# Attention of two blocks as one piece of work: pair tiles, one operation for both, another order of steps

## The chip, the cores and the metric

The kernel runs on one NeuronCore of a Trainium2 chip. The core has a matrix engine (TensorE, PE in the profile; PEld is its weight loading), three elementwise engines (VectorE = DVE, ScalarE = ACT, GpSimd = POOL), and SyncE (SP), which here issues every DMA, in program order. Each engine works through its own list in order and waits on semaphores. The metric is the device time of one launch in microseconds (us), lower is better.

## What is computed

A gated linear attention recurrence, and after it a feed-forward layer with squared ReLU, all in float32:

```python
# q, k, v, alpha: (B=4, H=8, S=768, D=48)
state = zeros(B, H, D, D)
for t in range(S):
    state = alpha[:, :, t, :, None] * state + einsum('bhd,bhe->bhde', k[:, :, t], v[:, :, t])
    y[:, :, t] = einsum('bhd,bhde->bhe', q[:, :, t], state)
x = y.transpose(0, 2, 1, 3).reshape(B * S, H * D)      # 3072 x 384
h = maximum(x @ w_in, 0)                               # w_in 384 x 2048, given as float64
out = h * h @ w_out                                    # w_out 2048 x 384, given as float64
```

## The kernel before

**Blocks and groups.** The sequence is cut into chunks of 128 steps; one chunk of one batch is a block. There are 24 blocks, block `n` being chunk `n // 4` of batch `n % 4`. Four blocks make a group (`GB = 4`), so six groups of 512 rows, and the feed-forward layer is computed group by group.

**Attention of a block.** `ln` takes the logarithm of alpha (ScalarE), from block 8 on `sp` splits it into two parts, `cs` sums along the chunk with a triangular matrix (TensorE), `eb` and `ei` exponentiate the sums with both signs (ScalarE), `mq` and `mk` scale q and k with them (VectorE), `turn` transposes both (TensorE) and `qc`, `kc` copy the result out (ScalarE). Then `scores` (L418) multiplies them in quarters of the array, `masked` (L426) keeps the lower triangle in a tile `am`, `state_sums` (L441) forms the products of k and v, and `sums_copied` (L452) makes `us`, the state at the middle of the chunk. `next_state` (L466, L467) makes the state for the next chunk; it needs `last`, the decay over the whole chunk, one column per head. From block 4 on `bl` stores the last row of the exponentials to DRAM and `br` fetches it back turned into columns, both by DMA; for blocks 0 to 3 `lt` and `lc` do it on TensorE and VectorE. The output products `y` (L398) come in two parts, `ga` and `gb`, since rows of the array change PSUM banks between them; `ev` copies y into `x` (L562).

**Pairs.** From block 4 on blocks go in pairs, with three short stretches of 64-wide matmuls between the layer's 128-wide ones: `turn` for both; `ga`: scores and sums of the first block, then the first part of the products of the pair before; `gb`: the second part of those products, then scores and sums of the second block. PSUM has eight banks, handed out in turn to all of these and to the layer's sums.

**The layer.** Group 0 multiplies float32 data directly (`ffn_in`, L931; L760 with `w_out`). Later groups use three passes over reduced-precision parts of weights (`wb`, `wl`, `wd`) and data (`xa`, `xl`, `xd`; `ha`, `hl`, `hd`): `in_x`, `in_y` (L681), then `turned_x`, `turned_y` (L843, L855) or `out_x`, `out_y` (L760). `splits_of_x` makes the parts of x in three column pieces. The parts `wl` and `wd` are kept in DRAM and streamed back by `pump` (L644) as long as fewer than `room` tiles are held.

**Weights.** They arrive as 64-bit floats in 16 pieces and are turned into float32 by `convert_first`, `convert_middle`, `convert_second` (L174 to L203).

**The order.** The first 30 us are a list written out by hand (`first`, L980): each word is a step and its block. `zeros2` (L384) is three matmuls on zeros whose result is not used, and `warm` (L244) is one more of that kind. `weights` loads the next piece of weights. `gt`, `gy`, `gk` hold the next load back until the transposes, the products or the sums of that block are done. After it, `weave` runs a list of units (layer matmuls, with a cost in units of its own) and slips in events at given times; `PLAN` (L996) gives the times of the attention steps within a pair, and `AT` (L19) every other constant. All of this fixes the order in which each engine and the DMA queue see their work.

## Time and profile before

| what | value |
|---|---|
| time, median of 3 runs | 516.4 us (515.83 to 516.55) |
| profiled execution, span from first to last instruction | 514.6 us |
| TensorE, weight load, VectorE, ScalarE busy | 508.3, 404.6, 377.0, 302.3 us |
| group 0, from the start to the first pass of group 1 | 0 to 124.5 us |
| groups 1 to 5, start of each | 124.5, 212.3, 291.7, 370.3, 444.9 us |
| last matmul of the chain ends | 510.9 us |
| DMA | 102.73 MB, mean 200 GB/s |
| granted TensorE clock | 1.00 |

The profile page gives busy times per engine, a chain of waits (what released what, followed back from the last instruction), and groups of equal instructions. A line of the chain or the timeline reads: start in us, length in us, engine, line of the kernel, what was written and read, how many. A bracket at its end is the idle time of that engine before it and who ended it. A float32 matmul leaves two records, so 16 score matmuls are 32.

### The profile page before, as it was taken

Reading aid. Unit: us, or ns where it says so; the run is one execution under the profiler, and the core shown is the slowest. Engines: PE = TensorE matmul, PEld = TensorE weight load, DVE = VectorE, ACT = ScalarE, POOL = GpSimd, SP = SyncE. Lnnn points to the kernel's source line nnn. Section 1 sums busy time; section 2 is a strip of 40 time slices with the busy share of each in tenths; the row PEclk is TensorE's granted clock in tenths of the full one; section 3 lists DMA queues with packets and bytes.
Section 4 is the critical chain, followed back from the end, with each engine's and each line's share of the span. In section 5 each row is a group of like instructions: output and inputs, shape, how many; then the busy total and the mean of one; then the engine's idle time right before and its main releaser. Section 6 shows DMA issues by size and latency. Waiting matters only on the chain.

```text
span 514.6 us, 12773 instructions
## 1 busy us (share of the span) xinstructions
PE 508.3 (99%) x5166; PEld 404.6 (79%) x5166; DVE 377.0 (73%) x656; ACT 302.3 (59%) x627; POOL 6.0 (1%) x33
## 2 busy tenths in 40 slices
PE   8999999999999999999999999999999999999997
PEld 6884456669877679988888888888888888888996
DVE  3798899898789869886698286799275588274961
ACT  4789875677788576376764175855075663144520
POOL 4000000000000000000000000000000000000000
PEclk9999999999999999999999999999999999999999
DMA  9989867272797788799975678894775544789201
GB/s 171 226 238 269 233 177 226 33 224 101 267 238 199 189 188 234 263 330 222 241 187 154 209 220 229 222 225 146 227 221 168 186 128 151 214 277 401 88 0 63
DMA packets 144794, 102.73 MB, mean 200 GB/s; under 512 B 116560, under 2 KB 118240, under 8 KB 144736
## 3 DMA queue, kind: packets, MB, share of 16 engines
q1 hardware_dynamic: 144736, 101.92, 70.4%
q8 instruction: 41, 0.67, 0.6%
q14 instruction: 17, 0.14, 0.1%
HBM read 84.57 MB, written 17.33 MB: 198 GB/s over the span
## 4 chain that ended last, share of the span: by engine, by line
PE 96%; DMA 2%; SPq 1%; DVE 1%; issue 0%; ACT 0%; DVEq 0%; POOLq 0%
PE h L681 31%; PE o L760 22%; PE o L843 13%; PE h L931 8%; PE o L855 6%; PE y L398 4%; PE sckv L418 3%; PE T L529 2%; PE sckv L441 2%; PE cs L288 1%; DMA a_in<-in_alpha_dram 1%; PE zeros L384 1%; DMA last<-row 1%; PE cs L291 1%; SPq L333 1%; PE cs L292 1%
## 5 line engine op out<-in xcount | busy, mean ns | idle before, releaser
L696 ACT ACTIVATE hid<-h 128x512 f32<-128x512 f32 x56 | 33.7, 601 | 88.4 <-PE h L681 86.7
L681 PE MATMUL h<-xd,wd 128*128 128x512 f32 x240 | 68.4, 398 | 0.0
L681 PE MATMUL h<-xa,wb 128*128 128x512 f32 x240 | 67.8, 391 | 0.0
L681 PE MATMUL h<-xl,wl 128*128 128x512 f32 x240 | 67.6, 390 | 0.0
L594 DVE TENSOR_TENSOR hid<-h,hid 128x512 f32<-128x512 f32 x56 | 38.5, 689 | 33.9 <-PE h L681 33.6
L562 ACT COPY x<-y 32x256 f32<-32x256 f32 (+1 forms) x137 | 48.9, 365 | 8.7 <-PE y L398 6.4
L681 PEld LDWEIGHTS h<-xl,wl 128*128 128x128 f32 x240 | 45.0, 188 | 9.6
L681 PEld LDWEIGHTS h<-xa,wb 128*128 128x128 f32 x240 | 44.9, 188 | 9.4
L681 PEld LDWEIGHTS h<-xd,wd 128*128 128x128 f32 x240 | 43.7, 188 | 9.2
L760 PE MATMUL o<-w_out,hid 128*128 128x384 f32 x144 | 48.9, 492 | 0.0
L931 PE MATMUL h<-x,w_in 128*128 128x512 f32 (+1 forms) x120 | 43.0, 511 | 0.0
L655 ACT ACTIVATE ha<-hid 128x512 fp32r<-128x512 f32 x42 | 26.7, 638 | 26.1 <-DVE hx L656 12.8
L760 PEld LDWEIGHTS o<-w_out,hid 128*128 128x128 f32 x144 | 26.7, 190 | 17.2
L710 DVE SCALAR_TENSOR_TENSOR hid<-hid 128x512 f32<-128x512 f32 x56 | 37.8, 684 | 0.0
L931 PEld LDWEIGHTS h<-x,w_in 128*128 128x128 f32 x120 | 22.4, 190 | 16.9 <-issue 13.9
L855 PE MATMUL o<-hd,wd 128*128 128x512 f32 x144 | 33.4, 391 | 0.0
L656 DVE SCALAR_TENSOR_TENSOR hl<-ha,hid 128x512 fp32r<-128x512 f32 x42 | 28.8, 686 | 4.7 <-ACT ha L655 4.4
L855 PEld LDWEIGHTS o<-hd,wd 128*128 128x128 f32 x144 | 26.8, 188 | 6.1 <-ACT o L848 0.6
L594 DVE TENSOR_TENSOR hd<-ha,hl 128x512 fp32r<-128x512 f32 x42 | 29.1, 692 | 1.9
L843 PE MATMUL o<-hx,wb 128*128 128x512 f32 x72 | 28.4, 394 | 0.0
L843 PE MATMUL o<-hx,wl 128*128 128x512 f32 x72 | 28.0, 389 | 0.0
L843 PE MATMUL o<-ha,wb 128*128 128x512 f32 x72 | 28.0, 389 | 0.0
(130 smaller groups left out, 950.4 us busy)
## 6 DMA issues: line engine op xcount, KB each, us to landing
wd<-do SPq DMA_DIRECT2D x37, 384.0 KB
wl<-lo SPq DMA_DIRECT2D x34, 384.0 KB
wl<-li SPq DMA_DIRECT2D x32, 384.0 KB
wd<-di SPq DMA_DIRECT2D x32, 384.0 KB
raw<-in_moe_w_in_dram SPq DMA_DIRECT2D x8, 768.0 KB
raw<-in_moe_w_out_dram SPq DMA_DIRECT2D x8, 768.0 KB
v_in<-in_v_dram SPq DMA_DIRECT2D x24, 192.0 KB
a_in<-in_alpha_dram SPq DMA_DIRECT2D x22, 192.0 KB
```

What stands on the lines that cost most here:

```text
L398: ins = nc.tensor.matmul(out=ys[e][64 * half : 64 * half + D + G * e, m % 2, p // 2, t], lhsT=lhsT, rhs=rhs, start=(half, e) not in seen, ...
L562: copy(out=x[kk][to : to + m, t : t + 2], in_=blk[n]["y"][e][r : r + m, :, p // 2],)
L594: nc.vector.tensor_tensor(out=o, in0=x, in1=z, op=op)
L655: nc.scalar.activation(out=a, in_=x, func=AF.Copy, scale=NEAR * E)
L656: nc.vector.scalar_tensor_tensor(out=l, in0=a.bitcast(FP32), scalar=-1.0 / E, in1=x, op0=ALU.mult, op1=ALU.add)
L681: nc.tensor.matmul(out=acc["h", j], lhsT=here[w, "i", p][:, kk, jj * 128 : (jj + 1) * 128], rhs=x_parts[x][:, kk], start=start and kk == 0 ...
L696: nc.scalar.activation(out=hid[j], in_=x, func=AF.Copy, scale=E)
L710: nc.vector.scalar_tensor_tensor(out=h, in0=h, scalar=0.0, in1=h, op0=ALU.max, op1=ALU.mult)
L760: nc.tensor.matmul(out=acc[t][:, 0:DM], lhsT=lhs[:, t * C : (t + 1) * C], rhs=rhs, start=start, stop=stop, skip_group_check=True,)
L843: nc.tensor.matmul(out=acc[c], lhsT=by_parts(here[w, "o", p], jj, c), rhs=x, start=n == 0 and w == "b", stop=n == NJ - 1 and w == "l", ski ...
L855: nc.tensor.matmul(out=acc[c], lhsT=by_parts(here["d", "o", p], n % 2, c), rhs=h_diff[n], start=False, stop=last and n == NJ - 1, skip_gro ...
L931: nc.tensor.matmul(out=ps, lhsT=w[:, kk, c0 : c0 + 128], rhs=xT[g][kk][:, cols], start=(kk == 0), stop=(kk == KM - 1),)
```

## The change

- The tiles of alpha, q, k and v hold two blocks side by side, as do the states (`s_two`), `us` (`u_two`) and the exponentials (`wide`, tags `b` and `i`, one buffer each, shared with the split parts of the logarithms).
- From block 4 on one operation serves both blocks of a pair: `pair_ln`, `pair_sp`, `pair_mq`, `pair_mk`, `pair_bl` and `pair_br` (one store and two fetches for each pair), `pair_masked`, `pair_states`.
- `ga` now does the scores and masks of both blocks and the first part of the products; `gb` the sums of both blocks, the second part of the products, and then the states of both.
- The sums of odd heads use 48 columns of k, where it was 64. States and `us` are handled on 112 partitions.
- The list `first` has another order and no `zeros`. `mq`, `mk`, scores and sums stay one block at a time there, and `us` is a copy, since the state before chunk 0 is zero. `st1` stands earlier, `v2` and `v3` are loaded after the second piece of weights. The marks stand before other loads: `gt1` (the transposes of block 1) now holds back the first piece of weights (before: `v2`), `gy0` (the products of blocks 0 and 1) the third piece (before: `v3`), `gk3` (the sums of block 3) `q4` (before: the third piece).
- `split_x` and `diff_x` treat all three column pieces in one operation.
- `PLAN` and `AT` have other times and constants; the pool `wt` has 25 buffers in place of 26, `room` is 24 in place of 26 and `room1` 24 in place of 25. `EARLY`, a second plan for blocks 4 to 7, is gone.
- Assertions (`needs`, `done`) on the order run while the program is built, not on the chip. `JOINED` is 0, so that what hangs on it isn't used.

The diff, cut to its core:

```diff
--- before.py
+++ after.py
-AT = {'u0': 2, 'evs': 0.4, 'lead': 4, 'post': 3, 'w_first': (45.82, 44.44, 94.99), 'wstep': 2.31, 'w_in_at': 1.92, 'w_in_by': 3.02, 'room1': 25, 'room': 26, 's0': 3, 'ahead': 12, 'late': 23, 'xs': 0.35, 'g0': (-0.17, 20.59, 27.02), 'sc0': (2.36, 2.26, 2.42), 'g1': (7.68, 18.74, 27.21), 'g': (2.3, 15.42), 'g1x': 47.42, 'gx': 39.86, 'g0x': 55.51, 'k0': 2, 'h0': 16, 'k1': 5, 'h1': 0, 'h1by': 5, 'evs0': 0.23, 'tp': 'DDAD', 'tp1': 'AADD', 'split': 8, 'o0': (42.39, 46.35), 'o1': (), 'o2': (21.54, 19.65, 30.49, 26.1, 43.38, 50.96), 'str1': 14.0, 'ga': 9.32, 'gb': 12.97}
+AT = {'lag': 2, 'joined': 0, 'tc': 0.02, 'u0': 2, 'evs': 0.41, 'lead': 5, 'post': 2, 'w_first': (46.95, 39.74, 97.6), 'wstep': 2.22, 'w_in_at': 1.73, 'w_in_by': 3.02, 'room1': 24, 'room': 24, 's0': 5, 'ahead': 11, 'late': 23, 'xs': 0.05, 'g0': (-0.17, 21.58, 26.97), 'sc0': (2.34, 2.19, 2.42), 'g1': (8.15, 17.47, 29.19), 'g': (2.87, 16.01), 'g1x': 49.26, 'gx': 40.98, 'g0x': 55.54, 'k0': 2, 'h0': 15, 'k1': 5, 'h1': 0, 'h1by': 2, 'evs0': 0.24, 'tp': 'DDAD', 'tp1': 'AADD', 'split': 8, 'o0': (40.85, 45.28), 'o1': (), 'o2': (20.9, 18.28, 30.52, 26.08, 42.67, 46.58), 'str1': 5.62, 'ga': 10.18, 'gb': 13.7}
...
-    s_all = kept("s", B + 2, [128, NP, 64])
-    u_all = kept("us", 3, [128, NP, 64])
+    s_two = kept("s", B // 2 + 1, [128, 2, NP, 64])
+    u_two = kept("us", 1, [128, 2, NP, 64])[0]
...
-        "a": kept("a_in", 2, [128, H * D]), "q": kept("q_in", 2, [128, H, 64]),
-        "k": kept("k_in", 3, [128, H, 64]), "v": kept("v_in", NV, [128, H * D]),
+        "a": kept("a_in", 1, [128, 2, H * D]), "q": kept("q_in", 1, [128, 2, H, 64]),
+        "k": kept("k_in", 2, [128, 2, H, 64]), "v": kept("v_in", NV // 2, [128, 2, H * D]),
     }
-    wt_pool = ctx.enter_context(tc.tile_pool(name="wt", bufs=26))
+    wt_pool = ctx.enter_context(tc.tile_pool(name="wt", bufs=25))
...
+    def pair_ln(n):
+        needs("load a", n, n + 1)
+        la = both(pair_of("a", n))
+        nc.scalar.activation(out=la, in_=la, func=AF.Ln)
+        for m in (n, n + 1):
+            blk[m]["la"] = tile_of("a", m)
 
...
+    def wide(name, dt=FP32):
+        return p2.tile([128, 2, H * D], dt, tag=name[0], name=name, bufs=1)
+
+    def pair_sp(n):
         if n < SPLIT:
             return
-        la = blk[n].pop("la")
-        hi = p2.tile([128, H * D], FP32R, tag="b", name="hi")
-        lo = p2.tile([128, H * D], FP32R, tag="inv", name="lo")
-        nc.vector.tensor_copy(out=hi, in_=la)
-        nc.vector.tensor_tensor(out=lo, in0=la, in1=hi.bitcast(FP32), op=ALU.subtract)
-        blk[n]["parts"] = hi, lo
+        la = both(pair_of("a", n))
+        hi, lo = wide("bhi", FP32R), wide("ilo", FP32R)
+        nc.vector.tensor_copy(out=both(hi), in_=la)
+        nc.vector.tensor_tensor(out=both(lo), in0=la, in1=both(hi).bitcast(FP32), op=ALU.subtract)
+        for i in range(2):
+            blk[n + i]["parts"] = hi[:, i], lo[:, i]
 
...
+        b = blk[n]["b2"] = blk[n - 1]["b2"] if n % 2 else wide("b")
+        nc.scalar.activation(out=b[:, n % 2], in_=sums_of_logs(n), func=AF.Exp)
...
+    def pair_scaled(x, n, factor):
+        needs("load " + x, n, n + 1)
+        needs("b" if x == "q" else "inv", n, n + 1)
+        done(x, n, n + 1)
+        t = pair_of(x, n)[:, :, :, 0:D]
+        nc.vector.tensor_tensor(
+            out=t, in0=t, in1=factor.rearrange("a m (h d) -> a m h d", h=H), op=ALU.mult
+        )
+
...
+    def pair_bl(n):
+        needs("b", n, n + 1)
+        done("row", n)
         if n // B < NCH - 1:
-            nc.sync.dma_start(out=rows_t[n], in_=blk[n]["b"][C - 1 : C].rearrange("a h d -> a (h d)"))
-
-    def br(n):
+            nc.sync.dma_start(out=rows_t[n], in_=blk[n]["b2"][C - 1 : C].rearrange("a m f -> a (m f)"))
+
+    def pair_br(n):
+        needs("row", n)
+        done("last", n, n + 1)
         if n // B < NCH - 1:
-            row = rows_t[n].rearrange("a (p e d) -> (a d) e p", e=2, d=D)
+            row = rows_t[n].rearrange("a (m p e d) -> (a d) e m p", m=2, e=2, d=D)
             for e in range(2):
-                nc.sync.dma_start(out=last_t[n % 4][64 * e : 64 * e + D, :], in_=row[:, e])
+                nc.sync.dma_start(
+                    out=last[64 * e : 64 * e + D, n % 4 : n % 4 + 2, :], in_=row[:, e]
+                )
 
...
+    def pair_scores(n):
+        ps = two["s", n] = [bank(n, "sc", (2, NP, 64)) for _ in range(2)]
+        for i in range(2):
+            ks, qs = blk[n + i]["ks"], blk[n + i]["qs"]
+            for p in range(NP):
+                for h in range(2):
+                    for e in range(2):
+                        rows = slice(64 * e, 64 * e + D)
+                        nc.tensor.matmul(
+                            out=ps[e][HALF[h], i, p, :], lhsT=ks[rows, p, HALF[h]],
+                            rhs=qs[rows, p, HALF[h]], start=True, stop=True, skip_group_check=True,
+                        )
+
+    def pair_masked(n):
+        needs("y", n - 4)
+        done("am", n, n + 1)
+        ps = two.pop(("s", n))
+        for e in range(2):
+            nc.vector.copy_predicated(
+                out=am_t[n // 2 % NAM][:, e].rearrange("a p t -> a (p t)").rearrange("a (p t) -> a p t", t=64),
+                data=ps[e].rearrange("a m p t -> a (m p) t"),
+                mask=halves_mask.bitcast(U32).unsqueeze(1).to_broadcast([128, 2 * NP, 64]),
+            )
+
+    def pair_sums(n):
+        needs("k", n, n + 1)
+        needs("load v", n, n + 1)
+        done("kv", n, n + 1)
+        ends = n // B == NCH - 1
+        ps = two["k", n] = [bank(n, "kv", (2, NP, 64)) for _ in range(1 if ends else 2)]
+        for i in range(2):
+            for p in range(NP):
+                for e in range(2):
+                    first, to = (2 * p + e) * D, D if e else 64
+                    for h in range(len(ps)):
+                        nc.tensor.matmul(
+                            out=ps[h][64 * e : 64 * e + to, i, p, G:64],
+                            lhsT=tile_of("k", n + i)[HALF[h], 2 * p + e, 0:to],
+                            rhs=tile_of("v", n + i)[HALF[h], first : first + D],
+                            start=True, stop=True, skip_group_check=True,
+                        )
+
+    def pair_states(n):
+        nonlocal spare
+        needs("y first", n - 2)
+        needs("st", n - 4)
+        needs("last", *([n, n + 1] if n // B < NCH - 1 else []))
+        done("st", n)
+        done("us", n, n + 1)
+        ps, i = two.pop(("k", n)), n % B // 2
+        old = s_two[i]
+        nc.vector.tensor_tensor(out=all_own(u_two), in0=all_own(ps[0]), in1=all_own(old), op=ALU.add)
+        for m in (n, n + 1):
+            blk[m]["u"], blk[m]["s"] = u_two[:, m % 2], old[:, m % 2]
+        if len(ps) > 1:
+            s_two[i], spare = spare, old
+            s = all_own(s_two[i])
+            by = rows_of(last)[:, n % 4 : n % 4 + 2, :].unsqueeze(3).to_broadcast([64 + D, 2, NP, D])
+            nc.vector.tensor_tensor(out=s, in0=all_own(ps[1]), in1=all_own(u_two), op=ALU.add)
+            nc.vector.tensor_tensor(out=s, in0=s, in1=by, op=ALU.mult)
 
...
+    def y_first(a):
+        needs("am", a, a + 1)
+        needs("us", a, a + 1)
+        done("y first", a)
+        product = y_begin(a)
+        for h in range(1 if a < B else 0, 2):
+            for m, p, e in heads(a):
+                rows = slice(64 * e, 64 * e + D)
+                s = blk[m]["u" if h else "s"]
+                product(m, p, e, s[rows, p, G * (1 - e) : 64], blk[m]["qs"][rows, p, HALF[h]], HALF[h])
+        for m, p, e in heads(a):
+            end = inner(product, m, p, e, e)
+        marks["y", a] = end
+        passed = nc.gpsimd.nop(nofuse=True)
+        dep(passed, end)
+        two["y"] = product, passed
+
+    def y_second(a):
+        done("y", a, a + 1)
+        product, passed = two.pop("y")
+        for i, (m, p, e) in enumerate(heads(a)):
+            begin = inner(product, m, p, e, 1 - e)
+            if i == 0:
+                dep(begin, passed)
+
...
+    def ga(a, n, t):
+        if t is not None and JOINED:
+            turn_and_copy(t)
         if n is not None:
-            for f in (scores, state_sums, masked, sums_copied):
-                f(n)
+            pair_scores(n)
+            pair_masked(n)
         if a is not None:
-            product = y_begin(a)
-            for h in range(1 if a < B else 0, 2):
-                for m, p, e in heads(a):
-                    rows = slice(64 * e, 64 * e + D)
-                    s = blk[m]["u" if h else "s"]
-                    product(m, p, e, s[rows, p, G * (1 - e) : 64], blk[m]["qs"][rows, p, HALF[h]], HALF[h])
-
-
-            for m, p, e in heads(a):
-                end = inner(product, m, p, e, e)
-            marks["y", a] = end
-            passed = nc.gpsimd.nop(nofuse=True)
-            dep(passed, end)
-            two["y"] = product, passed
+            y_first(a)
+
+    def gb(a, n, t):
+        if t is not None and JOINED:
+            turn_and_copy(t + 1)
         if n is not None:
-            next_state(n)
-
-    def gb(a, n):
-
+            pair_sums(n)
         if a is not None:
-            product, passed = two.pop("y")
-            for i, (m, p, e) in enumerate(heads(a)):
-                begin = inner(product, m, p, e, 1 - e)
-                if i == 0:
-                    dep(begin, passed)
+            y_second(a)
         if n is not None:
-            for f in (scores, state_sums, masked, sums_copied, next_state):
-                f(n + 1)
-
+            pair_states(n)
+
...
-    def split_x(g, kk):
-        if kk == 0:
-            x_parts["x"], x_parts["a"], x_parts["l"] = xT.pop(g), raw_r("xa"), raw_r("xl")
-        split_to(x_parts["a"][:, kk], x_parts["l"][:, kk], x_parts["x"][kk])
-
-    def diff_x(g, kk):
-        if kk == 0:
-            x_parts["d"] = raw_r("xd")
-        diff_to(*(x_parts[k][:, kk] for k in "dal"))
+    def split_x(g):
+        needs("x", GB * g, GB * g + 2)
+        x_parts["x"], x_parts["a"], x_parts["l"] = xT.pop(g), raw_r("xa"), raw_r("xl")
+        split_to(flat(x_parts["a"]), flat(x_parts["l"]), flat(x_parts["x"]))
+
+    def diff_x(g):
+        x_parts["d"] = raw_r("xd")
+        diff_to(*(flat(x_parts[k]) for k in "dal"))
 
...
-        zeros2 ln0 cs0 ln1 eb0 cs1 load0v ei0 mq0 mk0 load2a eb1 qT0 load3a qc0 mq1
-        kT0 kc0 load1v ei1 qT1 mk1 load2k load2q qc1 sc0 kT1 weights0 kc1 kv0 load3q
-        am0 lt1 sc1 ln2 us0 ln3 cs2 lt0 am1 load3k kv1 cs3 eb2 us1 ei2 gt1 mk2
-        load2v weights1 ya0 mq2 yb0 lc1 gy0 eb3 kT2 lc0 load3v qT2 ei3 load4a zeros2
-        st0 ea00 kc2 qc2 ed01 ed02 first0 zeros2 load4q mq3 zeros2 mk3 qT3 middle0
-        qc3 kT3 second0 first1 kc3 lt3 lt2 sc2 kv2 am2 ea03 us2 sc3 kv3 gk3 middle1
-        weights2 lc3 am3 us3 ha0 ya2 yb2 second1 weights3 ea20 lc2 ed21 ha1 ha3
-        weights4 ed22 ed23 first2 st2 middle2 ha2 hb0 load4v hb1 st3 st1 load4k
+        ln0 cs0 ei0 eb0 ln1 mq0 cs1 mk0 load0v qT0 eb1 load2a mq1 kT0 load3a load1v qc0 kc0
+        qT1 ei1 load2q qc1 load2k mk1 kT1 kc1 sc0 gt1 ln2 kv0 lt1 sc1 weights0 cs2 am1 ln3
+        am0 load3q us0 lt0 ei2 load3k kv1 us1 weights1 eb2 cs3 load2v lc1 eb3 ya0 lc0 mq2
+        yb0 load3v mk2 st0 st1 ei3 ea00 load4a gy0 kT2 qT2 qc2 first0 ed02 middle0 mq3 kc2
+        lt2 qT3 qc3 ed01 mk3 kT3 kc3 second0 ea03 lt3 sc2 kv2 first1 am2 middle1 us2 sc3
+        kv3 am3 us3 ha0 ya2 yb2 ea20 lc3 weights3 second1 weights2 ed21 ha1 first2 ed22
+        ed23 middle2 ha3 lc2 st2 st3 ha2 load4v load4k hb0 weights4 gk3 hb1 load4q
...
-        (-1.2, "ln0 ln1"),
-        (-0.5, "sp0"),
-        (0.0, "sp1"),
-        (2.5, "cs0 cs1 eb0 ei0"),
-        (3.0, "eb1 ei1"),
-        (3.5, "mk0"),
-        (4.0, "bl0"),
-        (4.5, "mq0 mk1 bl1"),
-        (5.0, "mq1"),
-        (6.5, "turn br1"),
-        (7.0, "kc0 qc0 kc1 qc1 br0"),
-        (9.5, "ga"),
-        (10.5, "gb"),
+        (-1.42, "pair_ln"),
+        (0.27, "pair_sp"),
+        (2.23, "cs0 cs1 eb0 ei0"),
+        (2.6, "eb1 ei1"),
+        (3.56, "pair_mk"),
+        (4.08, "pair_bl"),
+        (4.5, "pair_mq"),
+        (5.98, "pair_br"),
+        (6.75, "turn"),
+        (7.03, "kc0 qc0"),
+        (7.22, "kc1 qc1"),
+        (9.36, "ga"),
+        (10.29, "gb"),
     )
-    EARLY = (
-        (0, "ln0"),
-        (0.5, "ln1"),
-        (2.0, "cs0 eb0 ei0"),
-        (3.0, "cs1 eb1 ei1"),
-    ) + tuple(x for x in PLAN if x[0] > 3)
+    JOINED = AT["joined"]
```

## The prediction

> **What bounds the kernel now.** I read the page's engine totals first, then the chain of waits in order of time, then the timeline of the first 30 us.
>
> ```profile
> PE 508.3 (99%) x5166; PEld 404.6 (79%) x5166; DVE 377.0 (73%) x656; ACT 302.3 (59%) x627; POOL 6.0 (1%) x33
> ...
> PE 96%; DMA 2%; SPq 1%; DVE 1%; issue 0%; ACT 0%; DVEq 0%; POOLq 0%
> ```
>
> TensorE is the bound: the reader is to see 99% busy and 96% of the chain. So a saving on VectorE or ScalarE is worth something only where TensorE waits for it. The chain shows where that is:
>
> ```profile
> 18.49 0.44 PE qT L355 x4
> 18.92 3.89 PE zeros L384 x18
> 22.81 0.44 PE qT L355 x4
> ...
> 229.50 0.52 SPq L122
> 230.11 1.92 SPq L333
> ...
> 233.06 3.86 DMA last<-row
> 237.31 0.68 DVE hid L710
> 238.00 0.61 DVE hid L594
> 238.66 0.68 PE sckv L418 x28
> ...
> 444.94 32.64 PE h L681 x144
> ```
>
> The last line gives the steady rate, 32.64/144 = 0.227 us for one 128x512 pass. From 42 us on nearly every piece of the chain is TensorE at such a rate. The exceptions: at 238.14 two score records start and the rest only at 238.66 (0.52 us lost, because VectorE sat behind the fetch of `last`), and four hesitations near 144.5, 173.4, 181.4 and 182 us of 0.17 to 0.3, together 0.8. That makes 1.3 us of true waiting in 470. Before 42 us there is more: 3.89 us of `zeros`, matmuls whose result nobody uses, and the wait for the first loads.
>
> Are the fillers themselves the loss? The timeline of VectorE says what stood behind them:
>
> ```profile
> 15.26 0.36 DVE L452 TENSOR_TENSOR us<-sckv,s 128x192 f32<-128x192 f32 x1 [1.11 <-PE sckv L441]
> 18.74 1.33 DVE L562 COPY x<-y 64x256 f32<-64x256 f32 x3 [1.39 <-ACT x L562]
> 22.23 0.96 DVE L196 SCALAR_TENSOR_TENSOR power<-raw,power 128x768 uint32<-128x768 uint32 x1 [0.28 <-ACT power L187]
> 27.69 0.35 DVE L452 TENSOR_TENSOR us<-sckv,s 128x192 f32<-128x192 f32 x1
> 29.93 12.11 PE L931 MATMUL h<-x,w_in 128*128 128x256 f32 x48
> ```
>
> From `us1` (ends 15.62) to `us3` (ends 28.04) VectorE works in order with only two waits, 1.39 and 0.28. The second output product needs `us3`, and the long run of layer matmuls starts 1.89 us after it, at 29.93. So the first 30 us are set by VectorE's list, and the fillers lie beside it.
>
> **The change, part by part.**
>
> Pair operations. A scaling of 384 elements takes 0.55, a 512-element one of the same kind 0.69: about 1.05 ns an element, so one of 768 takes about 0.95 where two took 1.11. Over 10 pairs of `q` and `k` that is 3.2 us of VectorE. By the same slope the masks, the state operations, the splits of the logs and the splits of `x` (six VectorE operations of 0.68 into two of 1.73, five times) save some 14 more. ScalarE saves about 0.1 per pair of logarithms. All of it lies beside TensorE's 508 us: value 0. If that cover were gone it would be 17 us on VectorE's own path. What it buys is fewer hesitations.
>
> Scores in one stretch. Before, a first stretch is scores 0.62, sums 0.45, products 1.4 and a second 0.62, 0.46, 0.45; entering costs 0.09 and the first layer pass after it 0.14 more. After it there are still three stretches for each pair (turn, first, second) and as many matmuls. Inside a stretch scores and sums already follow each other at 32 records in 0.47. So 0. The odd heads' sums load 48 columns in place of 64 (a load of 120 against 134 ns), but products with 48 columns run 32 in 0.45 as well: between 0 and -0.02 a block, I take 0.
>
> States and the fetch of `last`. `pair_states` stands in the second stretch, behind the sums of both blocks; the fetch needs two DMAs in place of four, and the store one in place of two. The fetch took 3.86 us after a queue delay, VectorE waited 10.0 us for it in three places (longest 4.2). Now it is asked for at 5.98 units and needed at 13.7, about 10 us later at the chain's 1.3 us a unit. Behind that wait in VectorE's order stood the sums `hid` that free the bank for the scores. The 0.52 at 238 goes. Of the four other hesitations (0.8) I take half, 0.4, since the constants move them too; the bounds are 0.8 gained and 2 us of new ones (four times the 0.52). Middle: -0.9.
>
> What the pairs make later. The split parts and the exponentials of a pair share one buffer of two blocks, where each block had its own. So the first exponential waits for both cumulative sums, 0.35 us more (two passes of 0.18), on ScalarE, which idles 88 us before the copies of `h`: 0.
>
> The first list. No `zeros`, another order, and `st1` earlier (0.72, before at 33.6). I walk it with the row durations. The second load of `a` still lands at 6.9, so `cs1` starts at 7.47 as before; `kT1` comes before the first scores (10.9), the scores, sums and cumulative sums follow without a gap to 15.4, and `us1` ends near 15.6: nothing gained up to there. Then VectorE: two scalings 0.92, small copies 0.2, states 1.42, first halves of two weight pieces 2.0, copies of `x` 1.33, two scalings 0.92, second half 2.74, masks and sums 2.24: 11.7, of which 0.3 overlaps: 11.4, where it was 10.7 plus 1.67 of waiting. The 1.39 was for ScalarE's copies; now states and the weight piece stand before them, so I drop it and keep 0.28. `us3` then ends at 15.6 + 11.4 + 0.3 = 27.3 instead of 28.0: -0.7. Bounds: no wait at all, -1.0; all waits kept, +0.7. On SP's queue `v2`, `v3` go behind the second weight piece and `w2`, `w3` no longer wait for the sums of block 3. DMA had moved 4.24 MB by 22 us; what must have landed for `v3` is 4.7 MB without the gaps at 18 to 22 us, thus about 23 us, when the walk has TensorE at the sums of block 2. It holds, with less than a microsecond to spare.
>
> The fillers gone. Does the array stay at full rate without them? The granted clock reads 1.00 throughout, but starts do not:
>
> ```profile
> 4.25 1.06 PE L384 MATMUL zeros<-s 128*128 128x256 f32 x2
> ...
> 5.53 0.79 PE L384 MATMUL zeros<-s 128*128 128x256 f32 x2
> ...
> 19.19 1.03 PE L384 MATMUL zeros<-s 128*128 128x256 f32 x4
> 19.62 1.24 PE L384 MATMUL zeros<-s 128*128 128x256 f32 x5
> ```
>
> Early records start 0.427 apart (3.82, 4.25, 4.67, 5.10, 5.53), the later ones 0.215. Half rate lasts from 1.10 to about 5.5, 4.4 us of unbroken work. After the change the three warm-ups end near 4.0, the first cumulative sum starts at 4.25 and lasts, at half rate, to 5.5; then TensorE idles 2 us. I take it that full rate is reached as before: 0. Bound on the other side: half rate until about 15.7 costs half of 7.5 to 15.7, 4.1, less 1.0 of waits in that stretch: +3.1.
>
> [...]
>
> Fewer prefetched weight tiles (`room` 26 to 24, 25 to 24). No wait of TensorE on a weight load is in the list of waits. The loads of a layer's first tiles are issued at 356.7 and used from 371; two releases later is 361.8: 9 us are left. 0. Bound: two tiles late once, at 238 GB/s (240 to 257 us) 0.39 MB takes 1.65: +3.3.
>
> **Sum**: -0.7 - 0.9 = -1.6 against the span of 514.6; the median of the runs, 516.4, lies 1.8 above it. Forecast: span 513.0, time 514.8.
>
> **The rivals.**
> 1. The first list gains more: if VectorE's order lets TensorE take back most of the 3.89 us of `zeros` (against it: VectorE's 11.4 us of work). 3.0 + 0.9: 512.5.
> 2. Nothing to be seen: loads and VectorE hold the first 30 us, and the hesitations move elsewhere. For it: only 1.3 us of waits exist from 42 us on. 516.4.
> 3. Cold array: half rate to 15.7. For it: the sparse matmuls of 7 to 11 us. 514.8 + 3.1 = 517.9, slower. With half rate only to 12.3 it is 2.4 - 1.0 = 1.4: 516.2. It is slower from full rate later than about 13 us on.
> 4. Weight tiles late: 514.8 + 3.3 = 518.1, slower as soon as both tiles are late once; a single one, 1.65, is no change. Against it: the 9 us.
> 5. The change does not do what it says: the first stretch would not show 64 score records together. 516.4, together with rival 2.
>
> **How the numbers follow.** Forecast 0.42 (own range 514.0 to 515.9), rival 1 0.14, rivals 2 and 5 0.18, cold array 0.15, weight tiles or other new waits 0.11. A measurement here tells about 0.2% (1.0 us) from no change, so faster is 0.56, same 0.18, slower 0.26. The range runs from 512.3 (rival 1 with 0.2 to spare) to 518.2 (rivals 3 and 4).
>
> **What would show it.** `us3` ending at 27.3 and the long run of layer matmuls starting about 29.2; no wait of VectorE on `last`; no gap inside a score stretch; stage times from 42 us on unchanged but for 0.9. Wrong if 128x256 records or cumulative sums after 7.4 us start at the half-rate distance, if a weight load appears as a releaser of TensorE, or if the stages after 42 us differ by more than 1.5 us.

## The result and the profile after

The changed kernel is slower: a median of 523.9 us over 4 runs (521.9 to 526.2) against 516.5 us for the kernel before on the same chip, a ratio of 1.0143 with a 95% interval of 1.0118 to 1.0168. The profiled execution is the slowest of the four (526.2 us); its span is 524.2 us, 9.6 more than before. The forecast was 514.8 with a range of 512.3 to 518.2. Three executions of the experiments below lie far above the others of their kernel (531.9 us in run 7, 1772.6 in run 9, 521.1 in run 12), and the ratios leave them out.

The page's engine totals, the granted clock in 40 slices, and the DMA queues:

```profile
PE 509.9 (97%) x5142; PEld 405.4 (77%) x5142; DVE 373.4 (71%) x554; ACT 301.6 (58%) x607; POOL 5.5 (1%) x25
...
PEclk9889999999999999999999999999998999999999
...
q8 instruction: 40, 0.66, 0.5%
...
PE 95%; issue 1%; ACT 1%; DVE 0%; DVEq 0%; POOLq 0%
```

TensorE is busy 97% of the span, was 99%; the clock dips in slices 2, 3 and 31, where it was full throughout. The 24 records fewer are the `zeros`. VectorE lost 3.6 us and 102 instructions, not the 17 us that I worked out. And in the chain the share of "issue" goes from 0% to 1%: time in which TensorE waits for nothing that the profile shows. The chain of waits in order of time (start, length, what) says where:

```profile
18.22 1.66 issue
...
33.16 0.71 issue
...
35.12 11.84 PE h L1077 x48
...
175.30 1.08 issue
...
340.82 1.17 issue
...
397.59 2.10 issue
```

The long run of layer matmuls, at 29.93 before, starts at 35.1. VectorE's timeline has the two ends that the prediction named:

```profile
16.05 0.78 DVE L522 COPY us<-sckv 112x192 f32<-112x192 f32 x2
...
30.85 0.35 DVE L522 COPY us<-sckv 112x192 f32<-112x192 f32 x1
```

`us1` ends at 16.83 (before 15.62) and `us3` at 31.20 (before 28.04, predicted 27.3).

The span cut at six points that both kernels have (layer run, then each of the five groups), from the start times of the same matmuls, in us; the columns with numbers are experiments told below (records of added cheap matmuls; runs 1, 4, 3 and 12), each from its one profiled execution:

```
stage            before  after  24 rec.  44 rec.  88 rec.  44, warm middle
to layer run      29.93  35.05   31.83    31.99    34.89    29.14
to group 1        94.66  94.44   94.44    94.44    94.44    94.44
group 1           87.75  88.17   87.65    86.87    86.87    86.87
group 2           79.42  78.59   78.59    78.59    79.92    78.62
group 3           78.65  79.91   78.54    78.67    81.11    78.81
group 4           74.59  78.44   75.57    74.59    75.83    74.81
rest              65.55  65.54   65.55    65.55    65.55    65.55
```

So 5.1 of the 9.6 us are lost before the layer run; groups 1, 3 and 4 lose 0.4, 1.3 and 3.9, and the other stages win 1.1.

### The profile page after: what moved, and what is told of

It reads as the page before. It is cut to its first block, busy times and chain, and to the rows that moved or that the text cites. A ratio compares the mean times of both kernels' runs of the same rounds, so it can differ in the third digit from the quotient of the medians.

```text
span 524.2 us, 12521 instructions
## 1 busy us (share of the span) xinstructions
PE 509.9 (97%) x5142; PEld 405.4 (77%) x5142; DVE 373.4 (71%) x554; ACT 301.6 (58%) x607; POOL 5.5 (1%) x25
## 4 chain that ended last, share of the span: by engine, by line
PE 95%; issue 1%; ACT 1%; DVE 0%; DVEq 0%; POOLq 0%
PE h L824 32%; PE o L903 21%; PE o L987 13%; PE h L1077 8%; PE o L999 6%; PE y L455 5%; PE T L671 2%; PE sc L543 2%; PE kv L570 2%; PE cs L317 1%; PE sckv L475 1%; PE cs L320 1%; PE cs L321 1%; PE sckv L502 1%; PE kT L412 0%
## 5 line engine op out<-in xcount | busy, mean ns | idle before, releaser
L824 PE MATMUL h<-xa,wb 128*128 128x512 f32 x240 | 69.0, 396 | 0.0
L704 ACT COPY x<-y 32x256 f32<-32x256 f32 (+2 forms) x137 | 48.5, 365 | 28.0 <-PE y L455 25.8
L800 DVE SCALAR_TENSOR_TENSOR hx<-hx,hid 128x512 fp32r<-128x512 f32 x36 | 24.7, 686 | 9.0 <-ACT hx L799 9.0
```

The costliest lines, as they stand in the source:

```text
L704: copy(out=x[kk][to : to + m, t : t + 2], in_=blk[n]["y"][e][r : r + m, :, p // 2],)
L800: nc.vector.scalar_tensor_tensor(out=l, in0=a.bitcast(FP32), scalar=-1.0 / E, in1=x, op0=ALU.mult, op1=ALU.add)
L824: nc.tensor.matmul(out=acc["h", j], lhsT=here[w, "i", p][:, kk, jj * 128 : (jj + 1) * 128], rhs=x_parts[x][:, kk], start=start and kk == 0 ...
```

## What an "issue" stall is

TensorE's timeline around the last stall (start, busy, engine, line, operation, count; in brackets the idle time and its releaser):

```profile
395.15 1.16 PE L543 MATMUL sc<-qs,ks 48*64 48x64 f32 x64
396.13 0.65 PE L455 MATMUL y<-qs,s 48*48 48x64 f32 x32
396.57 0.65 PE L455 MATMUL y<-qs,us 48*48 48x64 f32 x31
...
397.03 0.56 PE L455 MATMUL y<-am,v_in 64*48 64x64 f32 x23
399.69 0.34 PE L455 MATMUL y<-am,v_in 64*48 64x64 f32 x8 [2.10 <-issue]
```

TensorE stops in the middle of one group of identical matmuls: 23 ran, 8 are left, and nothing that they read has changed. The list of waits names nothing else for these products: `y` waits for "issue" five times, 6.7 us in all. The trace's DMA queue q8 ("instruction") gives the other half. It moved 40 transfers of 16,384 bytes; TensorE issued 2 instructions (a weight load and a matmul) for each of 5,142 records, so 257 for each transfer. I read a transfer as a piece of TensorE's own program, of 256 instructions, some 128 records, and call the place between two pieces a boundary. The trace's counts are what it rests on: the five stalls (at records 219, 474, 1866, 3888 and 4393) come behind 449, 962, 3,778, 7,873 and 8,897 of the 10,427 instructions that the trace has for TensorE (143 of them are no records), and the distances, 513, 2,816, 4,095 and 1,024, are 2, 11, 16 and 4 times 256 to within one. For the stall shown, the boundary before it was crossed at 395.54; one q8 transfer ran from 397.27 to 398.38; TensorE went on at 399.69:

```profile
395.54:397.27 1.73, 1.73 (x136) 1.73 (x130) 1.62 (x4) 0.94 (x2) 0.00 (x0) 1.00 0.81 295
397.27:398.38 1.11, 0.32 (x22) 0.18 (x12) 0.44 (x1) 0.00 (x0) 0.00 (x0) 1.00 0.13 52
398.38:399.69 1.31, 0.00 (x1) 0.00 (x0) 0.00 (x0) 0.00 (x0) 0.00 (x0) 1.00 0.00 0
```

These are windows (length; busy time of PE, PEld, VectorE, ScalarE and GpSimd with counts; granted clock, DMA share, GB/s). In the first, TensorE uses up the piece while the DMA engines are 81% busy and the fetch has not begun; in the second the fetch runs beside almost nothing; in the third nothing runs at all, 1.31 us from the fetch's end to the next matmul.

**Theory F.** TensorE's program comes in pieces; the next is asked for when a boundary is crossed and can run some 3 to 6 us later; at the five stalls TensorE went on 6.1, 6.1, 3.2, 5.1 and 4.2 us after the boundary before. A stretch of 64-wide scores and products is 160 records in 2.5 us (169.80 to 172.29 in run 4), so a whole piece can be used up faster than the next comes. It stalls where a boundary falls into such a stretch with the previous boundary just ahead of it. The kernel before has such stretches too, but its 24 records of `zeros` put each later boundary 24 records earlier in the work. **Rivals**: R, the stalls belong to what the change does to the stages (one buffer for a pair, another order); W, it is only the warmth that the fillers gave.

## The experiments

**1. The boundaries moved by 24 records**, with matmuls that take next to no time (the 24 records 0.93 us, ahead of 1.13 us in which TensorE waits for `a_in`). The added step, called after the first cumulative sums:

```diff
+    def tiny(n):
+        ps = bank(n, "tiny", (2 * NP, 64))
+        x = s_two[1][:, 1].rearrange("a p d -> a (p d)")
+        for _ in range(12):
+            nc.tensor.matmul(out=ps[0:32, 0, 0:16], lhsT=x[:, 0:32], rhs=x[:, 0:16], start=True, stop=True)
...
-        ln0 cs0 ei0 eb0 ln1 ...
+        ln0 cs0 tiny2 ei0 eb0 ln1 ...
```

> The changed kernel with 12 tiny matmuls (32 columns by 16, 24 records of TensorE) after the first cumulative sums: they take almost no time and move every later boundary between two fetched pieces of TensorE's program (16,384 bytes, 256 instructions, 128 records) by 24 records, to where the kernel before has them. Theory F (TensorE outruns the fetch of its own program in the 64-wide score and product stretches): the stalls of 1.1 us at 175, 1.2 at 341 and 2.1 at 397 shrink to 0.4 or less each, the granted clock near 400 stays full, and the stages behind the first 35 us are 1 us shorter in all than before's; the first 35 us stay as in the changed kernel (layer run from about 35): 517 to 519 us. Rival R (the stalls come with what the change does to the stage, its single buffers or the order of its steps, wherever the boundaries lie): all three stay, 523 to 525.

517.1 us (10 runs), ratio 1.0014 (1.0001 to 1.0027). The stalls at 175 and 341 are gone. The one at 397 shrank from 2.3 to 0.95 between records (now at 392), not to 0.4, and one of 0.95 came at 194. Twelve matmuls whose result nobody uses took 6.9 us off the time. By the table, groups 1, 3 and 4 take 4.8 us less than in the changed kernel. Another 3.2 us are won ahead of the layer run, where I had expected nothing: the first stall is gone too, and the first four transposes start 0.11 us apart where they were 0.21. R falls for the later stalls: buffers and order are those of the changed kernel.

**2. The kernel before without its fillers.**

```diff
-        zeros2 ln0 cs0 ln1 eb0 ...
+        ln0 cs0 ln1 eb0 ...
...
-        load2v weights1 ya0 mq2 yb0 lc1 gy0 eb3 kT2 lc0 load3v qT2 ei3 load4a zeros2
-        st0 ea00 kc2 qc2 ed01 ed02 first0 zeros2 load4q mq3 zeros2 mk3 qT3 middle0
+        load2v weights1 ya0 mq2 yb0 lc1 gy0 eb3 kT2 lc0 load3v qT2 ei3 load4a
+        st0 ea00 kc2 qc2 ed01 ed02 first0 load4q mq3 mk3 qT3 middle0
```

> The kernel before without its four fillers of zeros and nothing else: its boundaries move to where the changed kernel has them. Theory F: stalls of 1 to 2 us appear in the kernel before too, in score and product stretches of the A kind near 170 and 390 where it has none now, beside a half-rate start: 519 to 524 us. Rival W (a cold start alone): about 3 us in the first 35 us and nothing behind them, 518 to 520. Rival R (fillers cost nothing to leave out, the stalls belong to the pairs): 514 to 517.

523.7 us, ratio 1.0131 (1.0088 to 1.0173): as slow as the changed kernel, with none of the pairs. Its profiled execution has a span of 523.2; of the 8.6 us that it loses, 4.5 lie ahead of the layer run (34.46) and 4.1 behind it, so W alone falls. Its timeline at 174.5:

```profile
174.46 0.57 PE L398 MATMUL y<-am,v_in 64*48 64x64 f32 x22
176.88 0.38 PE L398 MATMUL y<-am,v_in 64*64 64x64 f32 x9 [1.84 <-issue]
```

The same cut through one group. Of the two places that I named, one came within 5 us (expected 170); the other, 390, did not come, and 343 did with 0.8. The kernel before, with its fillers, already stood at the edge there, by its own timeline:

```profile
169.47 1.09 PE L398 MATMUL y<-qs,us 48*48 48x64 f32 x31
170.30 0.31 PE L398 MATMUL y<-am,v_in 64*48 64x64 f32 x4
```

31 records that take 0.65 elsewhere took 1.09, with a hole of 0.36 at a boundary, 1.43 after the end of a fetch.

**3. and 4. The dose.** The same step with 44 and with 22 tiny matmuls in place of 12 (two records each: 88 and 44).

> The changed kernel with 44 tiny matmuls (88 records) after the first cumulative sums, so the boundaries lie 88 records earlier in the work than in the changed kernel. Theory F, walked with TensorE's record times of the run with 24 tiny records and 3 to 4 us from one boundary until the next block can run: the stalls near 175 and 397 go, and five others of 1.1 to 2.1 us come near 101, 234, 257, 312 and 336 us (later by what went before), 5.6 to 11 us in all; with a first stretch of 32 to 35: 520 to 528 us. Rival R (the tiny matmuls help for another reason, such as keeping the array awake, and where the boundaries lie is nothing): no worse than with 12 of them, 516 to 519, and no stall at those five places.

> The same with 22 tiny matmuls (44 records). Theory F by the same walk: one stall of 1.2 to 2.2 us near 192 and none elsewhere behind the first 35 us; the layer run starts at 31 to 33; 515 to 517.5 us, about the same as with 24 records, a little less at best. Rival R: the more filler the better, or all alike; no stall at 192.

With 88 records 529.9 us (4 runs, 524.4 to 530.5), ratio 1.0235 (1.0183 to 1.0287), slower than expected; with 44 records 515.9 us (10 runs), ratio 0.9995 (0.9983 to 1.0007). More of the same filler is first good, then worse than none, as the walk said and the rival can't. The walk's places came in part. The profiled execution with 88, the fastest of its four, stops at two of the five (1.24 us at 262 and 2.18 at 344) and hesitates at a third (0.39 at 318); near 101 and 234 nothing stands. Its losses against 44 records are 2.9 us ahead of the layer run, with a stall of 2.3 at 18, and 5.0 in groups 2 to 4, of which 0.95 is a wait for a weight tile. With 44 the expected stall near 192 did not come: the fetch there ran from 190.19 to 191.41, begun 0.7 us ahead of the boundary's own record at 190.91, so the walk's 3 to 4 us were too long for that place. The pair stretch, whole, in that run:

```profile
169.80 1.16 PE L549 MATMUL sc<-qs,ks 48*64 48x64 f32 x64
170.78 0.65 PE L461 MATMUL y<-qs,s 48*48 48x64 f32 x32
171.23 0.65 PE L461 MATMUL y<-qs,us 48*48 48x64 f32 x31
...
171.69 0.68 PE L461 MATMUL y<-am,v_in 64*48 64x64 f32 x31
```

No idle time, and the next operation starts 2.5 us after the first score.

**5. The fillers back in the changed kernel**: `zeros2` at the front and after `qT2`, `ed02` and `mq3`.

> The changed kernel with four fillers of zeros again (24 records): one at the front, three in the first list near where the kernel before has them. Theory F: the boundaries behind the third filler stand where the kernel before has them, so the three later stalls shrink to 0.4 or less. With the warm start and the shift of the early boundary the layer run starts at 30 to 32; 511 to 515 us. Rival W alone (only warmth is lost with the fillers, the later stalls belong to the pairs): the first 35 us heal and the three stalls stay, 518 to 520. Rival R (neither depends on the fillers): 523 to 525.

522.3 us, ratio 1.0103 (1.0070 to 1.0136), not 511 to 515. The stalls at 175 and 341 went, as F says, and the one at 397 shrank to 0.69 between records; but one of 1.48 came at 197, and the layer run starts at 35.33, though the clock is full:

```profile
19.09 1.30 PE L455 MATMUL y<-am,v_in 64*64 64x64 f32 x49 [1.30 <-issue]
33.80 0.27 PE L455 MATMUL y<-qs,us 48*48 48x64 f32 x2 [2.26 <-issue]
```

Those are the two stalls of its first 35 us in TensorE's timeline, 1.5 and 2.5 us between records: 4.0 of the 5.4 by which the layer run is later than in the kernel before. Only the front filler, 6 records, stands ahead of the first two boundaries, and at the second the changed kernel's order puts its first products; 6 records are too few. So stalls alone, with a full clock, can cost most of what the first list lost. My expectation had overlooked that.

**6. and 7. Why the first fetch is late.** Its boundary is crossed at 13.77 and it begins at 17.40, 3.6 us later; at the three later stalls it is 0.8 to 2.2. First only the second piece of the weights was loaded later, then the first one too; TensorE's program is untouched.

```diff
-        am0 load3q us0 lt0 ei2 load3k kv1 us1 weights1 eb2 cs3 ...
-        yb0 load3v mk2 ...
+        am0 load3q us0 lt0 ei2 load3k kv1 us1 eb2 cs3 ...
+        yb0 load3v weights1 mk2 ...
```

> The changed kernel with one transfer issued later: the second piece of the weights (786 KB) behind the loads of v2 and v3 instead of ahead of them; TensorE's program is the same instruction for instruction. Theory F with the queue: the fetch of the program's next piece, which begins at 17.4 us behind that transfer though its boundary was crossed at 13.8, begins earlier; the stall of 1.9 us at 18.0 shrinks to 0.5 or less, the half-rate stretch of 10 us that follows it goes, the layer run starts at 30 to 31 instead of 35.1, and the three later stalls stay: 519 to 520 us. Rival W (the array falls to half rate because the four fillers are gone, with or without that stall): the layer run starts at 33 or later, 522 to 524.

No help: 524.3 us (4 runs), ratio 1.0144 (1.0108 to 1.0180); the fetch begins 3.9 us after the boundary, the stall is 2.1 between records, and the layer run starts at 36.06, where rival W had it. At the boundary (13.99) the first piece of the weights and the loads of q and k stood in the queue as before.

```diff
-        ... lt1 sc1 weights0 cs2 am1 ln3
-        am0 load3q us0 lt0 ei2 load3k kv1 us1 weights1 eb2 ...
-        yb0 load3v mk2 ...
+        ... lt1 sc1 cs2 am1 ln3
+        am0 load3q us0 lt0 ei2 load3k kv1 us1 weights0 eb2 ...
+        yb0 load3v weights1 mk2 ...
```

> The changed kernel with both early pieces of the weights (786 KB each) issued later: the first behind the loads of q and k of block 3, the second behind v2 and v3; TensorE's program is the same. Theory Q (the fetch of the next piece of the program waits for the transfers that stand in the DMA queues when its boundary is crossed, near 13.8; with the second weight piece alone moved, the first one and 0.4 MB of q and k still stood there): the fetch begins 1 to 2.5 us after the boundary instead of 3.6, the stall of 1.9 us at 18 shrinks to 0.9 or less, the three later stalls stay; 520 to 523 us, depending on when the weights arrive. Rival (the delay of the fetch has nothing to do with those transfers): it begins 3.2 us or more after the boundary, the stall is 1.5 or more, 523 to 526.

The fetch begins 1.4 us after the boundary, and the first stall is gone. In TensorE's timeline the group of 64 products runs in one go, where the changed kernel has 21 and 43 of them 1.66 us apart:

```profile
16.31 1.50 PE L455 MATMUL y<-am,v_in 64*48 64x64 f32 x64
...
22.22 1.12 PE L412 MATMUL qT<-ident,qk_lent 128*128 128x128 f32 x4 [3.02 <-DVE qk_lent L348]
```

The time is 523.6 all the same (4 runs), ratio 1.0126 (1.0093 to 1.0159), above the expected 520 to 523: the last line shows TensorE waiting 3.0 us for VectorE, behind the work on weights that now come late, and the stalls at 173, 339 and 396 stand as they were (1.3, 1.4 and 2.1 between records). This run also crossed its boundary 1.4 us earlier (12.41), since its first transposes ran at full rate, and the changed kernel's did not, with the same program. So it doesn't separate the loads from the moment. Two other runs, with loads in the changed kernel's order, speak for the loads: runs 4 and 11 cross this boundary 0.25 us after the first piece of the weights is issued, and the fetch begins 0.8 us after the boundary. The changed kernel and run 6 cross it 1.18 us after that issue, with the loads of q and k issued too, and the fetch begins 3.6 and 3.9 us after the boundary. So it is likely that transfers ahead of a fetch delay it, but no run shows this alone.

**8. and 9. What the fillers were for.** In the kernel before, every matmul of `zeros` cut to 32 columns by 16, then only two of the three fillers in the middle: records and boundaries stay, time and warmth go (18 of the cut records take 1.20 us, where the same 18 took 3.89).

```diff
-                out=ps[:, 0:NP, :], lhsT=s_t[3].rearrange("a p d -> a (p d)")[:, 0:128],
-                rhs=s_t[3], start=True, stop=True,
+                out=ps[0:32, 0, 0:16], lhsT=s_t[3].rearrange("a p d -> a (p d)")[:, 0:32],
+                rhs=s_t[3].rearrange("a p d -> a (p d)")[:, 0:16], start=True, stop=True,
```

> The kernel before with each matmul of zeros cut to 32 columns by 16: the same number of records at the same places, so the same boundaries, but next to no time and no warmth from them. Theory F: no stall behind the first 35 us and stages there as before within 0.3 us; what is lost without warmth alone shows in the first stretch: 0 to 2 us, 515 to 518. Rival W (the cold array is what the fillers guard against): half rate in the first 30 us and 3 to 5 us lost there, 519 to 521.

> The kernel before with two of its three fillers in the middle of the first list cut to 32 columns by 16 (same records, same boundaries), 2.6 us less of TensorE there. Theory (VectorE's list bounds the first 30 us, the boundaries are untouched): layer run at 29.5 to 30.5, stages behind as before within 0.3: 516 to 517 us, no change. Rival 1 (the fillers lie on the path): layer run at 27.5 to 29, 514 to 515.5. Rival 2 (the idle time halves the clock): layer run at 31 to 32, 517.5 to 519.

All cut: 519.4 us (10 runs), ratio 1.0054 (1.0029 to 1.0078), in rival W's band, though not all as W had it: the profiled execution, 518.1, has the layer run at 31.92, 2.0 us late and not 3 to 5, and no "issue" stall over 0.6. `us1` still ends at 15.65, so the front costs nothing here. The loss is in the middle, by windows (columns as above):

```profile
19.90:21.65 1.75, 0.18 (x7) 0.11 (x4) 1.75 (x5) 1.65 (x5) 0.00 (x0) 1.00 0.78 220
21.65:23.10 1.45, 1.45 (x15) 1.23 (x15) 1.17 (x2) 1.45 (x3) 0.00 (x0) 1.00 1.10 331
23.10:29.90 6.80, 6.80 (x139) 5.75 (x137) 6.60 (x14) 3.74 (x7) 0.00 (x0) 0.50 0.53 109
```

TensorE idles most of 1.75 us while VectorE works, and a little later the clock is half for 6.8 us although TensorE is busy throughout. Two of three cut: 516.5, ratio 1.0000 (0.9991 to 1.0009), clock full, layer run at 30.02. One filler of 6 records in the middle is enough, and the 2.6 us of TensorE taken away were free: VectorE's list is the bound there, as the prediction read it.

**10. to 12. A better version.** The boundaries of the 44 records, with real fillers among them: at all four places (10 tiny matmuls), at the front alone (19), and at the front and once before `qT3` (16). The last:

```diff
-        ln0 cs0 ei0 eb0 ln1 ...
+        zeros2 ln0 cs0 tiny2 ei0 eb0 ln1 ...
...
-        lt2 qT3 qc3 ed01 ...
+        lt2 zeros2 qT3 qc3 ed01 ...
```

> The changed kernel with its boundaries behind the first list where 44 records put them, and with real fillers: zeros at the front and at the three places in the first list, and 10 tiny matmuls after the first cumulative sums (26 records ahead of the first boundary). Theory F together with a warm start: no stall over 0.6 in the first 35 us, granted clock 1.00, layer run at 29.5 to 31; one stall of 1 to 2 near 192: 513 to 515.5 us, at or below the kernel before. Rival (the first list of the change is itself slower, whatever the clock and the fetches): layer run at 32 or later, 516 to 519.

> The changed kernel with one filler of zeros at the front (6 records) and 19 tiny matmuls (38 records) after the first cumulative sums: boundaries as with 44 records, a warm start, no filler in the middle of the first list. Theory: the second output block's `us1` ends near 15.8 as in the kernel before (18.3 with 44 tiny records alone), `us3` 11.2 us later at 27.0, the layer run starts at 29 to 30 (before 29.93) and the stages behind take 413.2 us instead of 415.1: 513 to 515 us, faster than the kernel before by 0.3 to 0.6%. Rival (the first list of the change needs the middle fillers too: the idle time of 1 to 2 us at 20 halves the clock): layer run at 31 to 32, 515.5 to 517.

> The same boundaries, with one filler of zeros at the front, 16 tiny matmuls (32 records), and one filler of zeros (1.3 us) where TensorE idles in the middle of the first list. Theory: as the run with the front filler alone where the idle time does no harm (within 0.5 us); 1 to 2 us less where it halves the clock: 513 to 515. Rival (any filler there delays the list, as 4 us of them seemed to): 0.5 to 1.5 us more than with the front filler alone.

All four places: 518.3 (516.4 to 521.3), in the rival's band; the profiled execution, the fastest of its ten, has the layer run at 31.41, with 4.05 us of `zeros` in the list and one stall of 0.86 at 29. Front alone: 516.0, layer run at 32.21; behind the idle time near 21 (1.05 and 0.35 us) the clock is half for 3.4 us, and a stall of 1.27 stands at 29: the rival of that expectation was right, and `us1` ends at 17.10, not near 15.8. Front and middle: **514.5 us** (12 runs), ratio 0.9965 (0.9950 to 0.9979), faster than both kernels. In the profiled execution the clock is full and no stall over 0.6 is left. VectorE's and TensorE's timelines:

```profile
26.91 0.35 DVE L528 COPY us<-sckv 112x192 f32<-112x192 f32 x1
```

```profile
19.77 1.56 PE L441 MATMUL zeros<-s 128*128 128x256 f32 x6
...
29.14 5.23 PE L1083 MATMUL h<-x,w_in 128*128 128x256 f32 x23
```

`us3` ends at 27.26, and the layer run starts at 29.14.

## Why the prediction was wrong

- **The step that failed is "The fillers gone: 0".** I costed the fillers' time and warmth, not their place in the program. Taking them out of the kernel before, and nothing else, cost 7.4 us (run 2); cutting only their time and keeping their records cost 2.9 (run 8). By the difference some 4.5 of the 7.4 are the moved boundaries and what follows their stalls. In the changed kernel, moving the boundaries back by 24 records of cheap matmuls gave 6.9 of the 7.4 us back (run 1).
- **Under it lay a premise**: the sum priced matmuls at their spacing and took it that TensorE always has its program at hand. In the kernel before the fetches were nearly hidden (the hole of 0.36 at 170.30, no stall over 0.6). In the changed kernel's profiled execution five were not: 7.8 us between records in all (1.9, 0.9, 1.3, 1.4 and 2.3), and after the first and the last of them half rate. No rival had this mechanism. "So 0" for the scores in one stretch isn't shown wrong: run 2 stalls without that stretch, and run 4 has it with no stall over 0.6.
- **Warmth** was mis-sized too. Rival 3 had half rate to 15.7 for 3.1 us. With the 22 tiny matmuls near the front the transposes ran at half distance until about 13.9 and `us1` ended 2.7 us late; in the changed kernel itself it was 1.2 us. This start is not set by TensorE's program alone: run 7 has the program of the changed kernel, and its transposes run at full rate from the first. Among the eight profiled kernels without a real filler at the front four start them at half distance (changed, 2, 4 and 6) and four at full (1, 3, 7 and 8); all six with one start at full. What costs more is the idle time near 20, which the fillers covered (run 8: 1.57 of idle time up to 21.65, then 6.8 us at half the clock) and which the prediction, looking only at the front, left out.
- **The first list, -0.7**, holds once this is out of the way: predicted `us3` at 27.3 and the layer run about 29.2; run 12 has 27.26 and 29.14. That it fits to 0.1 is in part luck: there `us1` ends at 16.12, 0.5 later than walked, and the way from it to `us3` takes 11.1 us where the walk had 11.7. In the changed kernel the two stand at 31.20 and 35.05.
- **The middle, -0.9**, had the right sign and half the size: without stalls (44 records) layer run to the end of group 4 takes 413.16 us against 415.07, -1.9: 0.2, 0.9 and 0.8 in the first three stages. No wait of VectorE on `last` is left in the changed kernel; before there were three, 10.0 us in all. How the gain divides among that, the four hesitations and the hole of 0.36 at 170.30 was not tried.
- **Pair operations, 0**: right in effect. The 17 us of VectorE were too many; its busy time fell by 3.6. The sum added up lengths of records, and neighbours overlap: before, two scalings of 0.55 start 0.46 apart (15.54 and 16.00), and one of the changed kernel, of 0.95, starts 0.86 ahead of the next operation (148.34 and 149.20).
- **Buffers of pairs, 0, and weight tiles, 0**: the changed kernel has no wait of TensorE on either. Rival 4 was seen once, 0.95 us on a weight tile in the run with 88 records.
- The signs I gave for being wrong did appear: half-rate distance after 7.4 us, and stages that differ by more than 1.5 us. What I had not listed was a stall inside a group of identical matmuls.

## What to carry to other kernels

Where TensorE runs more than a hundred records of small matmuls in some 2.5 us, look in the trace for the instruction queue's transfers and count records from one to the next: a stop inside a group of equal matmuls, a little over a microsecond after such a transfer ends (here 1.2 to 1.7 us), is by my reading of these runs the program arriving late. By the same reading an edit that adds or removes TensorE instructions ahead moves the later boundaries (here 24 records took away the stalls at 175 and 341 and brought one at 194), so a change is not judged from one alignment: try it with a few dozen cheap instructions more before you call it slower or faster. Here the same change measured from 0.35% faster to 2.35% slower by what stood in its first 22 us.

## What the runs showed that was not expected

- At its five stalls the changed kernel goes on 1.51, 1.32, 1.24, 1.43 and 1.31 us after the end of a 16,384-byte transfer on q8. Over the fourteen profiled kernels, 27 stops of over 0.6 us stood at such boundaries, and after each of them it was 1.2 to 1.7 us. Counted in TensorE's instructions, the 27 places all leave the same remainder when divided by 256, to within one. These transfers took 0.9 to 1.5 us, but for one of 2.2. From the boundary ahead to their start it was 2.2 to 4.1 us in the first 35 us, and 0.1 to 2.2 later. Away from the stops the count is looser: of all 570 transfers 199 begin ahead of the record at their boundary, by up to 8.2 us (in the kernel before and the changed one 28 of 81, by up to 4.2). So the record's start is not always the moment at which the next piece is asked for.
- The granted clock reads 1.00 from 4 to 14 us in the run with 44 records while four records of a transpose take 1.06 us, against 0.60 to 0.66 at full rate. The trace's first record of the clock in that run stands at 13.9 us, so the 1.00 ahead of it is not measured. It is the same in the changed kernel, where the first record stands at 10.80 and transposes start 0.213 us apart up to there and 0.11 behind it, and in the kernel before (5.90; 0.427 and 0.215), so the "1.00 throughout" of the prediction is no reading up to 5.90. There the spacing has to be read, not the clock.
- In the changed kernel one stop of 1.66 us at 18.2 was followed by half rate from 21.0 to 31.3, though TensorE was busy 97% of 22 to 30 (windows, columns as above):

```profile
18.00:20.00 2.00, 0.34 (x20) 0.20 (x13) 1.93 (x6) 0.16 (x1) 0.00 (x0) 1.00 0.53 73
...
22.00:30.00 8.00, 7.74 (x149) 6.64 (x147) 6.82 (x13) 7.08 (x14) 0.00 (x0) 0.50 1.03 286
```

  Of the 3.4 us ahead of it (17.6 to 21.0) TensorE was busy for 1.63. The half-rate stretches of this trace last 10.24 us (21.05 to 31.29) and 3.41 us (399.93 to 403.34, behind the stop of 2.10), that of run 8 lasts 6.8 and that of run 11 3.4. In the longest TensorE was busy for 9.98 of the 10.24 us before full rate came back. Behind the stops of 0.71, 1.08 and 1.17 us the clock stayed full, and so it did in run 5 (mean 1.000) with stops of 1.30 and 2.26: the length of a stop alone doesn't decide it, and what does is not shown.
